# Moving value differences and attention steps within a polysketch-attention and SwiGLU kernel

## The chip, the cores and the metric

The kernel runs on one core of a Trainium2 chip. A core has five engines with instruction queues of their own: TensorE (PE in the profile; its weight loads are listed as PEld), VectorE (DVE), ScalarE (ACT), GpSimd (POOL) and SyncE (SP, which here starts DMA transfers). Each works through its queue in order and waits on semaphores for the others. The metric is the device time of one execution in microseconds (us); lower is better.

## The reference

Two blocks follow each other. The first is attention with a polynomial sketch, over 4 batches, 4 heads, 1088 positions and a head dimension of 32; the second is a SwiGLU feed-forward block over the 4352 resulting tokens of 128 values, with 1536 hidden values.

```python
def phi(x):                                   # 32 values -> 64 features
    a = np.einsum('rd,bhsd->bhsr', S1, x)
    b = np.einsum('rd,bhsd->bhsr', S2, x)
    return np.einsum('bhsi,bhsj->bhsij', a, b).reshape(*x.shape[:-1], r * r)
q_p, k_p = (phi(q), phi(k))
kv = np.einsum('bhsf,bhsd->bhfd', k_p, v)     # per batch and head: 64 x 32
z = np.sum(k_p, axis=2)                       # per batch and head: 64
num = np.einsum('bhsf,bhfd->bhsd', q_p, kv)
den = np.einsum('bhsf,bhf->bhs', q_p, z)[..., None] + 1e-06
x = (num / den)                               # then (B,H,S,D) -> (B*S, H*D)
g = x @ w_gate
out = (g * (1 / (1 + np.exp(-g))) * (x @ w_val)) @ w_out
```

The sums over positions, kv and z, must be complete before any token of a batch is known, so the feed-forward block of a batch can only start when its attention is done.

## The kernel before, in words

**Tiling.** The tokens lie transposed in SBUF (xT, 128 values by 4352 tokens). Each batch is cut into three blocks of 384, 384 and 320 tokens, twelve blocks in all. The hidden dimension is cut into 12 chunks of 128. A *unit* is one block with one chunk: gate and value products, silu, and the multiplication of the two, which leaves one tile in the buffer hbuf. A *down* step (L943) multiplies one such tile by the output weights and adds it to the block's result in PSUM; after 12 of them the result is transposed and stored (L972).

**Stages.** Batch 0 comes first. Its 36 units are plain float32 products (function unit: products L912, silu L918, multiplication L929 on VectorE). Six early ones are *late* units: their value product is copied into hbuf by ScalarE, and the multiplication by the silu follows later on GpSimd (catch_up, L935). The loop over z runs the other thirty units; from z = 17 on, each is followed by a down step and by one part of attention. A closing loop then runs the remaining down steps of batch 0, three to a round, with parts of attention between them (its variable begun becomes true when batch 1's numerators are computed). From there on the *line* loop runs over y, 108 units of batches 1 to 3, with up to two down steps and a part of attention behind each.

**Split products in the line.** In the line the products are split into terms of a faster number format (function cut_unit). The weights are cut in advance by cut_weights, in four pieces of three chunks each, in four rows of steps: *first*, w1 = scaled copy on ScalarE; *low*, low = w - w1 (the value differences, on GpSimd for the value weights); *second*, wb = scaled low on ScalarE; *third*, wd = w1 - wb on GpSimd. All four are recorded at L849. Tokens are cut alike (L859, L860, L864 give x1, x0, xd). A line unit of the first kind then has the products xd by wd (L878), the plain gate product (L880), x1 by w1 (L884) and x0 by wb (L885); ScalarE copies the first scaled (L890), VectorE adds it to the sum of the last two (L893), ScalarE takes the silu (L897) and GpSimd multiplies (L902). From y = 22 (GATES) on the gate is split too; its weights are cut by VectorE in the line's first units.

**Attention of batches 1 to 3.** The generator attentions() yields after each small part, and parts_of(n) runs n parts. In order: transposes of keys (turn_keys, L309) and queries (L560), key sketches (L336), key features (L359), sums of features over the nine position groups (feature_sums, five GpSimd additions at L529, the last of which values() needs), key-value products (values(), L370 and L698 on TensorE), the fold and the spread of the result on VectorE (L583 to L708), query sketches (L324), query features and their transposes (L359, L742), and the numerators (L760), whose result goes to xT (L777). Parts that give TensorE a group of products in the line stand behind a mark "pe"; they run only where GROUPS names the unit y, and group() first runs any part still left before the mark.

**Order and buffers.** The order of instructions on each engine is written out by hand: it is the order of the calls. PSUM has eight banks. In the line one is held for the down steps, and the others go to whichever product comes next, oldest first, so a unit's first product waits for the reader of a bank filled three units before.

**The weights** arrive as 64-bit floats and are converted in 14 pieces; the last step of a piece is a multiplication at L270, on GpSimd for nearly all.

Of the kernel before, what the change touches and what calls it, by code (L numbers as in the profile page):

```python
# [19 lines left out]
def kernel(  # L20
# [126 lines left out]
    def load_k(b):  # L147
        nc.sync.dma_start(
            out=kld[:, 0:NX, :], in_=k[b].rearrange("h (pp x) d -> (h pp) x d", pp=32)
        )  # L150

    def load_q(b, x0=0, x1=NX):
        src = q[b].rearrange("h (pp x) d -> (h pp) x d", pp=32)
        nc.sync.dma_start(out=qld[:, x0:x1, :], in_=src[:, x0:x1, :])

    def load_v(b, queues):
        src = v[b].rearrange("h (pp x) d -> pp h x d", pp=32)
        for a, queue in enumerate(queues):
            n = min(NC, NX - NC * a)
            queue.dma_start(  # L160
                out=vld[32 * a : 32 * a + 32, :, 0:n, :],
                in_=src[:, :, NC * a : NC * a + n, :],
            )
# [620 lines left out]
    todo = []  # L784
# [33 lines left out]
    def cut_weights(w, lows, engine):  # L818

        rows = [], [], [], []  # L820
        sub = dict(op=ALU.subtract)
        for c, (w1, wb, wd) in enumerate(homes(w)):
            src = w[:, 3 * c : 3 * c + 3, :]
            low = lows[c]
            w_parts[id(w), c] = (w1, wb, wd)
            fine = dict(out=wd, in0=whole(w1), in1=whole(wb), **sub), engine.tensor_tensor
            if engine is nc.vector:
                fine = dict(
                    out=wd, in0=low, scalar=-BETA, in1=whole(w1), op0=ALU.mult, op1=ALU.add
                ), engine.scalar_tensor_tensor  # L830
            for row, f, args in zip(
                rows,
                (nc.scalar.activation, engine.tensor_tensor, nc.scalar.activation, fine[1]),
                (
                    dict(out=w1, in_=src, func=AF.Copy, scale=CUT),
                    dict(out=low, in0=src, in1=whole(w1), **sub),
                    dict(out=wb, in_=low, func=AF.Copy, scale=BETA),
                    fine[0],
                ),
            ):  # L840
                row.append((f, args))
        return rows

    def take(steps, n):

        for _ in range(n):
            if steps:
                f, args = steps.pop(0)
                f(**args)  # L849

    def cut_tokens(i, engine=nc.gpsimd):

        t0, n = blocks[i]
        x = xT[:, t0 : t0 + n]
        x1, x0, xd = x_parts[i] = [
            apool.tile([P, BW], F32R, tag=tag, name=name, bufs=2)
            for tag, name in (("qb", "x1"), ("dT", "x0"), ("rd", "xd"))
        ]
        nc.scalar.activation(x1[:, 0:n], x, AF.Copy, scale=CUT)  # L859
        engine.tensor_tensor(  # L860
            out=x0[:, 0:n], in0=x, in1=whole(x1[:, 0:n]), op=ALU.subtract
        )
        yield
        nc.vector.scalar_tensor_tensor(  # L864
            out=xd[:, 0:n], in0=whole(x0[:, 0:n]), scalar=-BETA, in1=whole(x1[:, 0:n]),
            op0=ALU.mult, op1=ALU.add,
        )
# [36 lines left out]
    def unit(i, j, late=False, between=(None, None)):  # L904


        t0, n = blocks[i]
        g, u = bank(), bank()
        for o, w in ((g, wg), (u, wv)):
            if between[0] and w is wv:  # L910
                between[0]()
            nc.tensor.matmul(  # L912
                o[:, 0:n], w[:, j, :], xT[:, t0 : t0 + n], start=True, stop=True
            )
        sg = fpool.tile(
            [P, BW], FP32, tag="sgl" if late else "sg", name="sg", bufs=6 if late else 5
        )
        nc.scalar.activation(sg[:, 0:n], g[:, 0:n], AF.Silu)  # L918
        slot_of[i, j] = slots.pop(0)
        hj = hbuf[:, slot_of[i, j], :]  # L920
        hidden[i, j] = hj
        todo.append((i, j))
        if late:
            if between[1]:
                between[1]()
            nc.scalar.copy(hj[:, 0:n], u[:, 0:n])
            lates.append((hj[:, 0:n], sg[:, 0:n]))
        else:
            nc.vector.tensor_tensor(  # L929
                out=hj[:, 0:n], in0=sg[:, 0:n], in1=u[:, 0:n], op=ALU.mult  # L930
            )

    def catch_up():
        o, sg = lates.pop(0)
        nc.gpsimd.tensor_tensor(out=o, in0=o, in1=sg, op=ALU.mult)  # L935

    def down():

        i, j = todo.pop(0)
        n = SPLIT if i == LAST else blocks[i][1]  # L940
        if j == 0:
            acc[i] = bank("g1" if i == 1 else "acc")
        nc.tensor.matmul(  # L943
            acc[i][:, 0:n],
            wo[:, j, :],
            hidden[i, j][:, 0:n],
            start=(j == 0),
            stop=(j == NCH - 1),
        )
        if i != LAST:  # L950
            hidden.pop((i, j))
            slots.append(slot_of[i, j])
        if j == NCH - 1:
            store(i, n)
# [34 lines left out]
    def part(name, i):  # L989

        next(fills[name, i], None)
# [97 lines left out]
    begun = [False]  # L1089

    def parts_of(n):

        for _ in range(n):
            if ahead[0] not in ("pe", "end"):
                ahead[0] = next(att, "end")
                begun[0] |= ahead[0] == "first"
# [48 lines left out]
    for z, (i, j) in enumerate(seq):  # L1145
        if z == 17:
            free_banks.pop()
            turn[0] %= 4
        unit(i, j)
        for p in parts.get(z, ()):  # L1150
            part(*p)
        if z in (24, 25, 26):
            catch_up()
        if z == 6:
            load_k(1)
            load_v(1, [nc.sync] * 4)
            load_q(1)
        if z >= 17:
            todo.remove(order[0])
            todo.insert(0, order.pop(0))  # L1160
            down()
        if z == 20:
            lows = [
                pool.tile([P, 3, P], FP32, tag=tag, name="low", bufs=bufs)[:]
                for pool, tag, bufs in ((apool, "qb", 2), (apool, "dT", 2), (apool, "rd", 2), (fpool, "sgl", 6))
            ]
            first, low, second, third = cut_weights(wv, lows, nc.gpsimd)
        if 20 <= z < 24:
            take(first, (2, 1, 1, 0)[z - 20])
            take(low, (0, 1, 2, 1)[z - 20])  # L1170
        if z in (25, 26):
            take(second, 2)
        if z >= 17:
            parts_of(1)
        if z == 26:
            take(third, 4)
    todo.sort()
    x_steps = None
    while todo:
        for _ in range(min(3, len(todo))):  # L1180
            down()
        if begun[0]:
            x_steps = x_steps or cut_tokens(HEAD, nc.vector)
            next(x_steps, None)
        parts_of(1 + begun[0] * (1 + (len(todo) < 3)))
    while not begun[0]:
        parts_of(1)
    run(x_steps or cut_tokens(HEAD, nc.vector))
# [4 lines left out]

    line = [3 * b + k for b in range(1, B) for k in ((0, 2, 1) if b == B - 1 else range(3))]
    END = len(line) * NCH
    GROUPS, GATES = (5, 7, 22, 24, 40), 22

    token_steps = {}
    for m, i in enumerate(line[1:], 1):
# [70 lines left out]
```

## Time and profile before

The time is the median of three runs: 295.32 us (295.3 to 296.36). The profiled execution spans 293.6 us.

| engine | busy us | share | instructions |
|---|---|---|---|
| TensorE (PE) | 282.3 | 96% | 2307 |
| VectorE (DVE) | 207.8 | 71% | 422 |
| ScalarE (ACT) | 181.9 | 62% | 432 |
| GpSimd (POOL) | 162.7 | 55% | 183 |

Busy times are of the engine as a whole; they say nothing of the stage that a change touches, so the work around it is read from the order in time. A line of that view gives the start, the duration, the engine, the kernel's line, the operation, the tiles (out<-in), the shape and how many instructions are merged; in square brackets, the idle time before it and the instruction that ended it. A float32 product counts as two instructions of TensorE. The chain of work that ended last lies to 83% on TensorE, 6% on VectorE and 5% on GpSimd. The batch-0 stage ends at about 97.5 us, where the line starts. From 95 to 110 us VectorE is busy for 14.50 of 15 us, from 180 us on TensorE for 109.59 of 113.6.

### The profile page before, as it was taken

How to read it: one execution, taken by the hardware profiler on the slowest of the kernel's cores; microseconds unless marked ns; L12 is line 12 of the kernel's file. 1: busy time of each engine (PE TensorE's matmuls, PEld its weight loads, DVE VectorE, ACT ScalarE, POOL GpSimd, SP SyncE). 2: the span in 40 equal slices, each digit the busy share in tenths (PEclk: the TensorE clock that was granted, in tenths of full speed). 3: DMA queues.
4: the chain of work that ended last, by engine and by line, in shares of the span. 5: the costliest groups of instructions: out<-in, count | busy, mean ns of one | idle time of the engine just before them, and what ended most of it. 6: DMA issues, size and time to landing. Idle time of an engine off the chain costs nothing.

```text
span 293.6 us, 6384 instructions
## 1 busy us (share of the span) xinstructions
PE 282.3 (96%) x2307; PEld 213.0 (73%) x2307; DVE 207.8 (71%) x422; ACT 181.9 (62%) x432; POOL 162.7 (55%) x183
## 2 busy tenths in 40 slices
PE   7899999996999799999999999999999999999994
PEld 6545566654656577767787778888888988888984
DVE  3997988873294996999568875656767666676751
ACT  3567565642301576555467777888888888888860
POOL 3315322269500695689836666557676666665650
PEclk9999999999799999999999999999999999999998
DMA  7563192302221033001001001001001010010101
GB/s 193 151 213 109 57 323 64 125 29 78 73 47 27 17 89 88 2 1 27 7 12 27 2 0 23 3 0 31 0 0 27 2 23 1 2 27 0 22 2 28
DMA packets 26144, 14.34 MB, mean 49 GB/s; under 512 B 19841, under 2 KB 24193, under 8 KB 26113
## 3 DMA queue, kind: packets, MB, share of 16 engines
q1 hardware_dynamic: 25456, 13.84, 18.1%
q8 instruction: 18, 0.29, 0.4%
q10 hardware_dynamic: 656, 0.10, 0.2%
q14 instruction: 14, 0.11, 0.1%
HBM read 11.41 MB, written 2.23 MB: 46 GB/s over the span
## 4 chain that ended last, share of the span: by engine, by line
PE 83%; DVE 6%; POOL 5%; ACT 2%; issue 2%; DMA 2%; SPq 0%; DVEq 0%; ACTq 0%
PE PS L943 25%; PE PS L912 14%; PE PS L884 10%; PE PS L878 10%; PE PS L885 10%; PE PS L880 4%; POOL zs L529 3%; PE PS L336 2%; PE PS L324 2%; PE PS L760 2%; DMA kld<-in_k_dram 2%; ACT sum L890 1%; PE PS L370 1%; DVE sum L893 1%; DVE phk L359 1%
## 5 line engine op out<-in xcount | busy, mean ns | idle before, releaser
L902 POOL TENSOR_TENSOR hbuf<-sg,sum 128x384 f32<-128x384 f32 (+1 forms) x107 | 109.8, 1030 | 58.9 <-ACT sg L897 50.6
L893 DVE SCALAR_TENSOR_TENSOR sum<-PS,sum 128x384 f32<-128x384 f32 (+1 forms) x192 | 93.9, 525 | 46.0 <-ACT sum L890 41.9
L943 PE MATMUL PS<-hbuf,wo 128*128 128x384 f32 (+2 forms) x288 | 103.6, 461 | 0.0
L890 ACT ACTIVATE sum<-PS 128x384 f32<-128x384 f32 (+1 forms) x192 | 80.5, 465 | 14.0 <-PE PS L878 13.6
L943 PEld LDWEIGHTS PS<-hbuf,wo 128*128 128x128 f32 x288 | 52.3, 190 | 10.6 <-issue 0.8
L897 ACT ACTIVATE sg<-sum 128x384 f32<-128x384 f32 (+1 forms) x85 | 42.7, 503 | 26.8 <-DVE sum L893 26.8
L878 PE MATMUL PS<-xd,gphq 128*128 128x384 f32 (+1 forms) x85 | 47.9, 564 | 0.0
L884 PE MATMUL PS<-x,w 128*128 128x384 f32 (+1 forms) x107 | 42.2, 395 | 0.1
L878 PE MATMUL PS<-xd,wd 128*128 128x384 f32 (+1 forms) x107 | 39.4, 368 | 1.8 <-POOL zs L529 1.5
L885 PE MATMUL PS<-x,wb 128*128 128x384 f32 (+1 forms) x107 | 35.0, 327 | 0.0
L918 ACT ACTIVATE sg<-PS 128x384 f32<-128x384 f32 (+1 forms) x37 | 17.4, 473 | 24.5 <-PE PS L912 22.9
L912 PE MATMUL PS<-xT,wg 128*128 128x384 f32 (+1 forms) x74 | 30.1, 489 | 0.0
L912 PE MATMUL PS<-xT,wv 128*128 128x384 f32 (+1 forms) x74 | 29.4, 479 | 0.2 <-DVE wv L270 0.2
L878 PEld LDWEIGHTS PS<-xd,wd 128*128 128x128 f32 x107 | 20.3, 189 | 12.6 <-POOL zs L529 1.7
L884 PE MATMUL PS<-x,graw 128*128 128x384 f32 (+1 forms) x85 | 27.8, 328 | 0.0
L885 PE MATMUL PS<-x,graw 128*128 128x384 f32 (+1 forms) x85 | 27.6, 325 | 0.0
L929 DVE TENSOR_TENSOR hbuf<-sg,PS 128x384 f32<-128x384 f32 (+1 forms) x31 | 16.2, 526 | 12.3 <-PE PS L912 12.0
L884 PEld LDWEIGHTS PS<-x,w 128*128 128x128 f32 x107 | 20.1, 188 | 4.2 <-ACT sum L890 0.4
L878 PEld LDWEIGHTS PS<-xd,gphq 128*128 128x128 f32 x85 | 16.1, 189 | 8.6 <-issue 0.4
L885 PEld LDWEIGHTS PS<-x,wb 128*128 128x128 f32 x107 | 20.2, 188 | 2.9
L912 PEld LDWEIGHTS PS<-xT,wv 128*128 128x128 f32 x74 | 14.1, 194 | 9.4 <-DVE hbuf L929 0.9
L912 PEld LDWEIGHTS PS<-xT,wg 128*128 128x128 f32 x74 | 13.5, 193 | 9.3 <-issue 1.2
(130 smaller groups left out, 345.4 us busy)
## 6 DMA issues: line engine op xcount, KB each, us to landing
kld<-in_k_dram SPq DMA_DIRECT2D x4, 544.0 KB, 4.4
vld<-in_v_dram SPq DMA_DIRECT2D x12, 144.0 KB, 4.8
qld<-in_q_dram SPq DMA_DIRECT2D x3, 544.0 KB, 3.8
raw<-in_moe_w_out_dram SPq DMA_DIRECT2D x4, 384.0 KB, 4.0
out_dram<-o SPq DMA_DIRECT2D x28, 48.0 KB, 1.8
raw<-in_moe_w_gate_dram SPq DMA_DIRECT2D x3, 384.0 KB, 3.2
raw<-in_moe_w_val_dram SPq DMA_DIRECT2D x3, 384.0 KB, 3.4
out_dram<-o SPq DMA_DIRECT2D x16, 40.0 KB, 1.7
```

Of the source, the lines that this page charges most:

```text
L878: nc.tensor.matmul(d, wd, xd, start=True, stop=True)
L880: nc.tensor.matmul(g, wg[:, j, :], xT[:, t0 : t0 + n], start=True, stop=True)
L884: nc.tensor.matmul(p, w1, x1, start=True, stop=False)
L885: nc.tensor.matmul(p, wb, x0, start=False, stop=True)
L890: nc.scalar.activation(s, d, AF.Copy, scale=-1.0 / BETA)
L893: nc.vector.scalar_tensor_tensor(out=s, in0=p, scalar=1.0 + 1.0 / BETA, in1=s, op0=ALU.mult, op1=ALU.add)
L897: nc.scalar.activation(sg, sums[0] if both else g, AF.Silu)
L902: nc.gpsimd.tensor_tensor(out=hj[:, 0:n], in0=sg, in1=sums[-1], op=ALU.mult)
L912: nc.tensor.matmul(o[:, 0:n], w[:, j, :], xT[:, t0 : t0 + n], start=True, stop=True)
L918: nc.scalar.activation(sg[:, 0:n], g[:, 0:n], AF.Silu)
L929: nc.vector.tensor_tensor(out=hj[:, 0:n], in0=sg[:, 0:n], in1=u[:, 0:n], op=ALU.mult)
L943: nc.tensor.matmul(acc[i][:, 0:n], wo[:, j, :], hidden[i, j][:, 0:n], start=(j == 0), stop=(j == NCH - 1),)
```

## The change

Four edits, all of order. No tile, shape or operation changes.

The value differences are rearranged in the last units of the z loop. Before: the first scaled copies at z = 20 to 22, the differences (low) one at z = 21, two at 22, one at 23, the second copies two at z = 25 and two at 26, and all second differences (third) at z = 26. After: the first copies two at z = 20 and two at 21, three differences at z = 21; three second copies at z = 25; the fourth difference at z = 26, behind the last late multiplication; three second differences there; and the fourth second copy and second difference at z = 29. The aim is that the sums of batch 1's features, which stand behind these differences on GpSimd, start sooner.

In the closing loop the last two rounds of down steps each ran three parts of attention; they now run one each. What this leaves over (transposes of keys and queries of later batches, and the sums of batch 2's features) runs in the line's first units, one part behind each, and the first two groups of the line's attention move from units 5 and 7 to 6 and 8. The aim is that the first units' own work on VectorE comes earlier.

```diff
             first, low, second, third = cut_weights(wv, lows, nc.gpsimd)
-        if 20 <= z < 24:
-            take(first, (2, 1, 1, 0)[z - 20])
-            take(low, (0, 1, 2, 1)[z - 20])
-        if z in (25, 26):
-            take(second, 2)
+        if z in (20, 21):
+            take(first, 2)
+        if z == 21:
+            take(low, 3)
+        if z == 25:
+            take(second, 3)
         if z >= 17:
             parts_of(1)
         if z == 26:
-            take(third, 4)
+            take(low, 1)
+            take(third, 3)
+        if z == 29:
+            take(second, 1)
+            take(third, 1)
...
-        parts_of(1 + begun[0] * (1 + (len(todo) < 3)))
+        parts_of(1 + (begun[0] and len(todo) > 2))
...
-    GROUPS, GATES = (5, 7, 22, 24, 40), 22
+    GROUPS, GATES = (6, 8, 22, 24, 40), 22
```

## The prediction

> **What bounds the kernel now.** I read the page first, then the list of waits, then the order in time of each engine round the two waits of TensorE on GpSimd. Times are us from the start of the profile before (the "old clock").
>
> ```profile
> PE 282.3 (96%) x2307; PEld 213.0 (73%) x2307; DVE 207.8 (71%) x422; ACT 181.9 (62%) x432; POOL 162.7 (55%) x183
> PEclk9999999999799999999999999999999999999998
> ```
>
> TensorE is the bound: 282.3 of 293.6. What a change of order can win is its 11.3 us of idle time, and time in which its clock is low: one slice in forty shows a 7.
>
> ```profile
> PE PS L698 <- POOL zs L529: 2.5, 1, 2.5
> PE PS L878 <- POOL zs L529: 1.5, 1, 1.5
> ```
>
> The largest waits of TensorE are the two that the change aims at. The first, in order of time:
>
> ```profile
> 68.00 1.21 PE L370 MATMUL PS<-phk,vld 128*32 128x64 f32 x72
> 71.66 0.32 PE L698 MATMUL PS<-zs,ones 128*32 128x64 f32 x8 [2.45 <-POOL zs L529]
> 71.91 1.27 PE L336 MATMUL PS<-s,kT 128*64 128x64 f32 x36
> 73.11 1.44 PE L912 MATMUL PS<-xT,wg 128*128 128x320 f32 x2
> 74.34 1.27 PE L912 MATMUL PS<-xT,wv 128*128 128x320 f32 x2
> 75.41 1.38 PE L943 MATMUL PS<-hbuf,wo 128*128 128x384 f32 x2
> 76.72 1.69 PE L324 MATMUL PS<-s,qT 128*32 128x96 f32 x72
> ```
>
> TensorE ends the key-value products of batch 1 at 69.2 and stands still for 2.45. The three pairs from 73.11 then take 3.61; the same pairs take 0.64 + 0.54 + 0.64 = 1.82 five us later (78.34 to 80.16). The stretches say why (third column from the end: clock):
>
> ```profile
> 73.00:74.00 1.00, 1.00 (x9) 0.73 (x5) 0.77 (x2) 0.00 (x0) 1.00 (x2) 0.57 0.00 0
> 75.00:76.00 1.00, 1.00 (x3) 0.55 (x2) 0.28 (x1) 0.02 (x1) 1.00 (x2) 0.50 0.16 33
> 77.00:78.00 1.00, 1.00 (x61) 1.00 (x56) 0.00 (x0) 0.18 (x1) 0.35 (x1) 1.00 0.11 22
> ```
>
> Half clock from about 73.1 to 76.5, right behind the standstill. What GpSimd did ahead of it:
>
> ```profile
> 57.00 1.01 POOL L849 TENSOR_TENSOR low<-wv,w 128x384 f32<-128x384 f32 x1
> 61.37 1.00 POOL L270 TENSOR_TENSOR wo<-man,exp 128x384 f32<-128x384 f32 x1 [3.36 <-DVE man L261]
> 62.33 2.92 POOL L849 TENSOR_TENSOR low<-wv,w 128x384 f32<-128x384 f32 x3
> 65.20 1.01 POOL L935 TENSOR_TENSOR hbuf<-hbuf,sg 128x384 f32<-128x384 f32 x1
> 66.16 2.51 POOL L529 TENSOR_TENSOR zs<-phk 128x512 f32<-128x512 f32 x2
> ```
>
> It idles 3.36 before the conversion of the last output weights, then does three value differences ahead of the feature sums. The second wait:
>
> ```profile
> 97.25 1.76 DVE L359 TENSOR_TENSOR phk<-kab 128x512 f32<-128x512 f32 x1
> 98.94 1.42 DVE L309 STREAM_TRANSPOSE kT<-kld 128x640 f32<-128x640 f32 x2
> 100.69 1.39 DVE L560 STREAM_TRANSPOSE qT<-qld 128x640 f32<-128x640 f32 x2
> 102.01 0.98 DVE L893 SCALAR_TENSOR_TENSOR sum<-PS,sum 128x384 f32<-128x384 f32 x2
> ```
>
> The view names GpSimd here, but L878 at 102.67 (fourth unit of the line, U3) writes a bank that the first unit's sum (L893) must have read; that sum was ready at 98.9 and ran at 102.01, behind five instructions of attention. So this wait is VectorE's order, 1.46 us.
>
> **What the Trainium skill says.** "TensorE: Matmul & The Clock Gate", Part 1, "What's actually happening": the array falls to half clock after an idle window of about 3.4 us and returns after a busy one; the windows run freely. The trace agrees: 3.4 us at half clock. Same page, "Architectural detail": ACT and DVE are strict FIFO; the late sum shows it. "GPSIMD Engine Reference", 1 "Specifications": its SBUF interface is shared with VectorE instructions that have two SBUF inputs. The trace agrees: the 128x512 key features took 0.68 with GpSimd still, and 1.76 beside a feature sum.
>
> **Part 1: differences one unit sooner.** No instruction is added or removed; the order on ScalarE and GpSimd changes. Differences 2 and 3 move ahead of the L270 conversion. Their inputs (L849 on ScalarE) are done at 56.0 and 56.95, so they run at 57.97 and 58.95 in the idle 3.36, free. L270 still starts at 61.37 (its input comes at 61.28), and the late multiplication L935 follows at 62.33, not 65.20. Features for the sums are ready at 62.47 and 63.54, in time. From L935's start to the last sum's end the old order took 71.61 - 65.20 = 6.41; so 62.33 + 6.41 = 68.74, and TensorE asks at 69.2: the 2.45 goes whole, with 0.46 to spare. Behind it TensorE sets the pace to 97.5: the fold on VectorE, the query sketches and the numerators (16 down products of 10 us hide the feature chain; it ended 1.9 before TensorE asked) all move with it. With the standstill gone, the small products last 68.0 to 70.65; the like stretch at 105.2 to 107.6 ran at full clock. So the half clock goes too: 3.61 - 1.82 = 1.79. **Sum 4.24.** Bounds: 2.45 if the clock dips anyway, 4.24 if not; I take 4.24.
>
> The fourth difference, its ScalarE scaling and its second difference move behind the late multiplications: about 70.6, 76.6 and 77.1. Their reader is the tenth unit of the line, past 110, and GpSimd idled 19.68 there: nothing. The fourth scaling on ScalarE sits in its 11.43 of idle before the numerators: nothing.
>
> **Part 2: fewer parts in the last rounds, groups one unit later.** The last two rounds ran 3 + 3 parts and now run 1 + 1; key and query transposes and feature sums spread over the line's units 0 to 2. On the old clock (all of it now 4.24 earlier): the first feature sum on GpSimd now waits for the last key features. These end at 97.95 (0.68 instead of 1.76, GpSimd being still). VectorE goes on: output transpose 0.47 to 98.4, keys 0.80 to 99.15, sum U0 0.55 to 99.7, keys 0.7, sum U1 to 100.85, queries 0.8, gate difference 0.85 (L849), sum U2 to 102.85. U3 finds its bank at 101.06, so the 1.46 goes. U3, U4, U5 at 1.17 each (98.72 to 99.89 is one) end at 104.57; the key-value products (1.03) end at 105.6.
>
> There a **new wait** begins. Sums of features and multiplications (L902) alternate on GpSimd: sum 98.05 to 99.4; multiplication to 100.8; sum 1.3 to 102.1; multiplication 1.0; sum 1.3 to 104.4; multiplication 1.0 to 1.3; sums 0.72 + 0.72: ends at 106.9 to 107.3. And L336 of the group now waits for the sum of U5: from 102.85, queries 0.62, gate 0.85, then three times sum and gate (0.47 + 0.85, pipelined) less the last gate, about 107.3. So TensorE idles 1.3 to 1.7 at L698, L336 starts at about 107.45 and unit U6 at 107.45 + 1.2 = 108.65. The old U6 started at 108.89. **Gain 0.24**, not 1.46: VectorE was busy 14.50 of 15 from 95 to 110, so it, not the one wait, sets this stage. Bounds: if gate differences run as L860 does beside a still GpSimd (0.56), 4 x 0.3 less, U6 at 107.5, gain 1.3; if multiplications take 1.34 as at 103.3, loss 0.3. From U8 on (114.7) both orders have done the same products.
>
> Batch 2's feature and query parts then come one unit (1.82) later against the line, and the third group stays at unit 22. Feature sums end about 139.5, asked for at 143.0; the last query transpose ends about 139.5, asked for at 140.48: hidden. The sum of unit 21, whose bank L760 takes, ended at 140.56 and now follows that transpose, a sum and an xd (0.55 to 1.05): 140.2 to 141.5. Loss 0 to 0.9; I take 0.3.
>
> **Sum:** 4.24 + 0.24 - 0.3 = 4.2; 295.3 - 4.2 = **291.1**.
>
> **Rivals.** *The clock follows the new wait* (16%): 1.3 to 1.7 idle among 2.4 us of small products is near what came before the dip at 73 (2.45 idle); a further 1.8 is lost: 292.9. For it: nearness. Against: 1.46 idle at 101.2 left the clock at 1.00. *VectorE gains more* (8%): 291.1 less 1.1, 290.0. For it: the key features save 1.08 by a still GpSimd. Against: GpSimd is busy beside the gate differences. *No change* (7%): the clock dips at 73 all the same and both losses reach their ends, 295.3 - 2.45 + 0.3 + 0.9 = 294.1. *Slower* (5%): multiplications between the sums take 1.72 each (the slowest L902), U6 comes 2.1 later, half clock there and at 73 too, 0.9 at unit 22: 295.3 - 2.45 + 2.1 + 1.8 + 0.9 = 297.7. For it: the sums now really stand behind multiplications that wait for VectorE. Against: everything must go wrong at once. My forecast: 64%.
>
> **How the numbers follow.** The time is the forecast's. The range takes in its bounds (4.24 + 1.3 gives 289.8; 0.3 and 0.9 lost gives 292.3) and the clock rival at 292.9: 289.9 to 293.1. Faster by over 0.5% means below 293.8: 64 + 16 + 8 = 88%; same 7%; slower 5%.
>
> **What would show it.** No wait of L698 near 67 to 69 and no 7 in the clock's row; L912 pairs behind it at 0.54 to 0.64; key features at 0.68 each near 93; no wait of L878 near 97; instead about 1.5 of L698 on GpSimd near 101, and under 1 at L760 near 136. Wrong if the clock still halves for 3.4 us in either place, or if the new wait at L698 is over 2.5.

## The result, and the profile after

The changed kernel takes **291.88 us** (median of four runs: 291.78, 291.84, 291.92 and 293.83), the kernel before 295.31 (four runs beside them, 294.97 to 296.36). The ratio is 0.9894, 95% interval 0.9846 to 0.9941. The profiled execution spans 289.9, before 293.6. "Old clock", U0, U1 and so on, "first group" (L370, L698, L336) and "second group" (L324) are used as in the prediction; "third group" is the L370 at unit 22.

The page of the kernel after, its busy times and clock row:

```profile
PE 280.7 (97%) x2307; PEld 212.4 (73%) x2307; DVE 207.1 (71%) x422; ACT 181.5 (63%) x432; POOL 162.7 (56%) x183
PEclk9999999999999999999999999999999999999999
```

The 7 has gone from the clock row. TensorE's busy time fell by 1.6 for the same 2307 instructions, about what the half clock had cost. The list of waits of the kernel after still has one of 2.3 at L698:

```profile
PE PS L698 <- POOL zs L529: 2.3, 1, 2.3
```

But it is not the one of before. TensorE in order of time, where the old wait stood:

```profile
67.65 1.21 PE L370 MATMUL PS<-phk,vld 128*32 128x64 f32 x72
68.68 0.29 PE L698 MATMUL PS<-zs,ones 128*32 128x64 f32 x8
68.91 1.27 PE L336 MATMUL PS<-s,kT 128*64 128x64 f32 x36
70.10 0.81 PE L912 MATMUL PS<-xT,wg 128*128 128x320 f32 x2
70.75 0.70 PE L912 MATMUL PS<-xT,wv 128*128 128x320 f32 x2
71.28 0.81 PE L943 MATMUL PS<-hbuf,wo 128*128 128x384 f32 x2
```

No bracket stands at L698: the list shows no wait of it. The three pairs start 0.65 and 0.53 apart, and the next product starts at 72.02: 1.92 in all, where they took 3.61. GpSimd ahead of it, kernel after:

```profile
56.64 2.91 POOL L849 TENSOR_TENSOR low<-wv,w 128x384 f32<-128x384 f32 x3
61.01 1.00 POOL L270 TENSOR_TENSOR wo<-man,exp 128x384 f32<-128x384 f32 x1 [1.46 <-DVE man L261]
61.98 1.00 POOL L935 TENSOR_TENSOR hbuf<-hbuf,sg 128x384 f32<-128x384 f32 x1
...
67.67 0.73 POOL L529 TENSOR_TENSOR zs<-zs,phk 128x256 f32<-128x256 f32 x1
```

Three differences in one row fill part of the idle time, which was 3.36 and is now 1.46; the last sum ends at 68.40, 0.28 before L698 starts.

The new wait is in the line. TensorE, kernel after:

```profile
100.62 1.21 PE L370 MATMUL PS<-phk,vld 128*32 128x64 f32 x72
104.16 0.32 PE L698 MATMUL PS<-zs,ones 128*32 128x64 f32 x8 [2.33 <-POOL zs L529]
104.41 1.27 PE L336 MATMUL PS<-s,kT 128*64 128x64 f32 x36
```

Points on the way split the span:

| from the profiles, us | before | after |
|---|---|---|
| U0 starts (L878) | 97.48 | 92.78 |
| U0 to U8 | 17.22 | 18.92 |
| of it U0 to U6 | 11.41 | 12.83 |
| U8 to the third group | 27.28 | 27.18 |
| third group to the last row of products (L958) | 144.34 | 144.33 |

So 4.70 is gained before the line (0.36 of it by loads that came sooner in this execution, ahead of everything that was changed), 1.70 is given back in the line's first eight units, and behind them nothing moves. The last products come 3.1 sooner; the other 0.6 of the span lies behind the last copy (o_last, at 289.63 and at 286.52), in the last transfers: 4.0 before, 3.4 after. What follows asks why the line gave back 1.7.

### The profile page after: what moved, and what is told of

Its sections match the earlier page's. It is cut to its first block, busy times and chain, and to the rows that moved or that the text cites. A ratio compares the mean times of both kernels' runs of the same rounds, so it can differ in the third digit from the quotient of the medians.

```text
span 289.9 us, 6382 instructions
## 1 busy us (share of the span) xinstructions
PE 280.7 (97%) x2307; PEld 212.4 (73%) x2307; DVE 207.1 (71%) x422; ACT 181.5 (63%) x432; POOL 162.7 (56%) x183
## 3 DMA queue, kind: packets, MB, share of 16 engines
HBM read 11.41 MB, written 2.23 MB: 47 GB/s over the span
## 4 chain that ended last, share of the span: by engine, by line
PE 84%; DVE 6%; POOL 3%; ACT 2%; issue 2%; DMA 1%; SPq 0%; DVEq 0%; POOLq 0%; ACTq 0%
PE PS L943 26%; PE PS L912 16%; PE PS L884 10%; PE PS L878 10%; PE PS L885 10%; PE PS L880 4%; PE PS L336 2%; PE PS L324 2%; PE PS L760 2%; POOL zs L529 2%; DVE sum L893 1%; DMA kld<-in_k_dram 1%; ACT sum L890 1%; PE PS L370 1%; POOL hbuf L902 1%
## 5 line engine op out<-in xcount | busy, mean ns | idle before, releaser
L902 POOL TENSOR_TENSOR hbuf<-sg,sum 128x384 f32<-128x384 f32 (+1 forms) x107 | 109.4, 1025 | 61.4 <-ACT sg L897 51.2
L893 DVE SCALAR_TENSOR_TENSOR sum<-PS,sum 128x384 f32<-128x384 f32 (+1 forms) x192 | 93.9, 526 | 48.3 <-ACT sum L890 42.1
L878 PE MATMUL PS<-xd,gphq 128*128 128x384 f32 (+1 forms) x85 | 47.9, 564 | 0.0
L878 PE MATMUL PS<-xd,wd 128*128 128x384 f32 (+1 forms) x107 | 39.4, 369 | 0.7 <-DVE sum L893 0.4
L912 PE MATMUL PS<-xT,wg 128*128 128x384 f32 (+1 forms) x74 | 29.5, 480 | 0.0
L912 PE MATMUL PS<-xT,wv 128*128 128x384 f32 (+1 forms) x74 | 28.8, 471 | 0.2 <-DVE wv L270 0.2
L878 PEld LDWEIGHTS PS<-xd,wd 128*128 128x128 f32 x107 | 20.3, 189 | 11.5 <-DVE sum L893 1.2
L878 PEld LDWEIGHTS PS<-xd,gphq 128*128 128x128 f32 x85 | 16.1, 189 | 8.6 <-issue 0.4
```

The costliest lines, as they stand in the source:

```text
L878: nc.tensor.matmul(d, wd, xd, start=True, stop=True)
L893: nc.vector.scalar_tensor_tensor(out=s, in0=p, scalar=1.0 + 1.0 / BETA, in1=s, op0=ALU.mult, op1=ALU.add)
L902: nc.gpsimd.tensor_tensor(out=hj[:, 0:n], in0=sg, in1=sums[-1], op=ALU.mult)
L912: nc.tensor.matmul(o[:, 0:n], w[:, j, :], xT[:, t0 : t0 + n], start=True, stop=True)
```

## The experiments

Each kernel was timed beside the kernel before, and its ratio is to that.

### The two parts by themselves

Part 1 alone is the kernel after with two lines as before:

```diff
-        parts_of(1 + (begun[0] and len(todo) > 2))
+        parts_of(1 + begun[0] * (1 + (len(todo) < 3)))
-    GROUPS, GATES = (6, 8, 22, 24, 40), 22
+    GROUPS, GATES = (5, 7, 22, 24, 40), 22
```

> Part 1 alone: the value differences moved, the closing loop and the groups as before. Theory A (part 1 is the whole gain, and part 2 costs about 1.6 us at the first group of the line): no wait of L698 and no half clock near 70, U0 of the line about 4.3 sooner, the old 1.46 us wait of L878 back, no wait of L698 in the line; 290.3 to 291.0 us. Theory B (part 2 brings what it was meant to, and part 1 less than it seems): 293.0 us or more.

Measured: **290.52** (290.22 to 291.66), ratio 0.9851 (0.9812 to 0.9891). U0 starts at 93.33, and U0 to U8 takes 17.23 as before. In its first units GpSimd does all five sums in a row. The wait at L878 stays; its line names GpSimd, but as in the kernel before, the product follows VectorE's sum of U0 (L893, from 97.86). TensorE, then GpSimd, of part 1 alone:

```profile
98.52 0.42 PE L878 MATMUL PS<-xd,wd 128*128 128x384 f32 x1 [1.45 <-POOL zs L529]
```

```profile
96.30 2.09 POOL L529 TENSOR_TENSOR zs<-zs 128x512 f32<-128x512 f32 x2
98.47 0.73 POOL L529 TENSOR_TENSOR zs<-zs,phk 128x256 f32<-128x256 f32 x1
99.16 5.18 POOL L902 TENSOR_TENSOR hbuf<-sg,sum 128x384 f32<-128x384 f32 x4
```

The sums are done at 99.20, then come the multiplications (L902). Part 1 is the whole gain: without part 2 the kernel is no slower.

Part 2 alone is the kernel before with those two lines as after.

> Part 2 alone: the value differences as before, fewer parts in the last rounds and groups at units 6 and 8. Theory A: the 2.45 us wait and the half clock at 68 to 77 are there, and the first group of the line waits over 2 us for the feature sums; 296.5 to 297.2 us, slower than before. Theory B: 293.8 us, faster than before by the 1.46 us of the wait of L878.

Measured: **297.13** (296.11 to 298.0), ratio 1.0052 (1.0023 to 1.0082): part 2 makes the kernel slower. Its fourteen runs fall into two heaps, seven at 296.1 to 296.6 with a mean clock of 0.994 and seven at 297.7 to 298.0 with 0.988. The profile is of the second kind; the first group's wait of 2.33 is followed by half clock. TensorE, and the stretches round it (third column from the end: clock):

```profile
108.61 0.32 PE L698 MATMUL PS<-zs,ones 128*32 128x64 f32 x8 [2.33 <-POOL zs L529]
```

```profile
105.00:110.00 5.00, 2.67 (x117) 2.34 (x116) 4.91 (x11) 1.08 (x3) 4.92 (x6) 1.00 0.35 111
110.00:115.00 5.00, 5.00 (x19) 3.39 (x13) 1.11 (x3) 2.25 (x6) 3.89 (x4) 0.66 0.11 24
```

The first of the two rows also shows VectorE (4.91 of 5) and GpSimd (4.92) full round L698.

### The two edits of part 2 apart

Part 1 with the closing loop of after alone:

> Part 1 and, of part 2, the fewer parts in the last rounds alone; the groups stay at units 5 and 7. If the groups' later place is what makes the alternating sums bearable: L698 waits 3 to 4 us for the feature sums, which end near 104 whatever TensorE does; 293.0 us, or near 295 where the clock halves behind it. If the place does not matter: 291.9 us as the changed kernel.

Measured: **295.03** (294.35 to 296.09), ratio 0.9982 (0.9963 to 1.0002). The sums lie between multiplications as in the kernel after, and the group asks a unit sooner. On TensorE:

```profile
99.67 1.21 PE L370 MATMUL PS<-phk,vld 128*32 128x64 f32 x72 [0.39 <-DVE sum L893]
104.56 0.44 PE L698 MATMUL PS<-zs,ones 128*32 128x64 f32 x8 [3.69 <-POOL zs L529]
104.93 2.19 PE L336 MATMUL PS<-s,kT 128*64 128x64 f32 x36
```

A wait of 3.69, then half clock at once (2.19 for products that take 1.27), in every one of its fourteen runs, to judge by their mean clock (0.994 or less).

Part 1 with the groups of after alone:

> Part 1 with the first two groups of the line's attention one unit later (6 and 8), and the closing loop as before. Theory A (what part 2 loses comes from the closing loop, which puts the feature sums behind the line's multiplications; the place of the group alone costs nothing when the sums are early): no wait of L698 in the line, the wait of 1.45 at L878 stays, U0 to U8 about 17.2, and 290.3 to 290.8, as for part 1 alone (290.52). Rival B (the later groups are what costs, since batch 2's features and queries then stand later against the line): a wait of 0.5 or more ahead of the third group at unit 22 or within the groups, and 291.3 to 292.

Measured: **291.2** (291.01 to 291.46), ratio 0.985 (0.9811 to 0.9889). In its profile the group's place does cost something: U0 to U8 takes 17.95, 0.72 more than with part 1 alone, of which 0.47 shows as a wait of L336 for VectorE's sum of the unit before it:

```profile
103.76 1.27 PE L336 MATMUL PS<-s,kT 128*64 128x64 f32 x36 [0.47 <-DVE sum L893]
```

The kernels with the old line (before, part 1 alone, and the filled one below) agree to 0.01 in this distance, so 0.72 is clear of noise there. The medians differ by 0.7 as well, but the ratios (0.985 and 0.9851) do not. So the two edits belong together: the later group costs up to 0.7, and keeps the loop's edit from costing 4.5; with both, 1.4 is lost.

### Are the multiplications between the sums the cause?

The kernel after with all five sums of batch 2 issued to GpSimd ahead of the line:

```diff
-        yield from beside(turn_keys(3), sums)
-        yield from beside(turn_queries(2), sums)
+        while sums:
+            sums.pop(0)()
+        yield from turn_keys(3)
+        yield from turn_queries(2)
```

> The changed kernel, with batch 2's five feature sums all issued ahead of the line, right behind the features, and only the transposes left in the units 0 to 2. Theory A1 (the group waits because the sums alternate with the multiplications on GpSimd, and nothing else): the sums end near 99, L698 does not wait, U6 starts about 2 us sooner; 289.8 us. Theory A2 (VectorE's queue sets it as well): L698 does not wait, but L336 of the group then waits for the sum of U5, which ran at 103.45 in the changed kernel; U6 starts at most 0.5 us sooner; 291.4 to 291.9 us.

Measured: **291.08** (290.83 to 292.54), ratio 0.9863 (0.9822 to 0.9904). The wait of L698 is gone, but the next product of the group has one of its own (TensorE; this kernel's lines stand 2 further down):

```profile
103.48 1.27 PE L336 MATMUL PS<-s,kT 128*64 128x64 f32 x36 [1.86 <-DVE sum L895]
```

VectorE's sum of U5 ends at 103.43. In the kernel after it ends at 103.99 and GpSimd's last sum at 104.11: two queues end the stage at nearly the same time, and taking one away shows the other. In this execution the clock halved behind the wait of 1.86; it is the 292.54, the only one of seven.

The same with the gate differences (VectorE, L849) moved behind the group, and the two later rows of gate steps with them:

```diff
-            if y >= (0, 1, 5, 5)[n]:
+            if y >= (0, 5, 6, 7)[n]:
```

> The changed kernel with the feature sums issued ahead of the line, and the gate differences on VectorE moved from units 1 to 4 to units 5 to 8 (and the steps behind them to 6 to 10). If VectorE's queue is what the first group waits for: no wait of L336 over 0.3 us, U6 1.6 us sooner. Whether that stays a gain is what the run decides: the moved 3.5 us meet the features of batch 3 at units 9 to 13, where the sum of unit 14 came only 0.6 us ahead of need. Gain kept: 289.5 us; moved into waits of L878 at units 14 to 18: 290.5 to 291.5 us.

Measured: **290.69** (290.45 to 292.08), ratio 0.9837 (0.9809 to 0.9865). The first group has no wait left and U0 to U8 takes 15.71, 1.5 less than before. But U8 to the third group takes 29.08 instead of 27.2. The stretch from 105 to 135 (behind its length: busy PE, PEld, DVE, ACT, POOL) has VectorE busy for 27.29 of 30 us, against 24.30 in the kernel after, and TensorE waits twice for it (0.35 and 0.46):

```profile
105.00:135.00 30.00, 29.18 (x177) 20.11 (x176) 27.29 (x41) 16.91 (x36) 21.23 (x18) 1.00 0.13 29
```

So VectorE's queue did bound the first group; but the work put off fills it up to unit 22 and is waited for there.

### GpSimd and VectorE beside each other

The prediction let the last key features run alone on VectorE (0.68). In the kernel after they took, on VectorE and GpSimd:

```profile
92.55 1.77 DVE L359 TENSOR_TENSOR phk<-kab 128x512 f32<-128x512 f32 x1
97.65 1.08 DVE L849 TENSOR_TENSOR hbuf<-wg,graw 128x384 f32<-128x384 f32 x1
99.75 1.50 DVE L849 TENSOR_TENSOR hbuf<-wg,graw 128x384 f32<-128x384 f32 x1
```

```profile
92.34 1.43 POOL L529 TENSOR_TENSOR zs<-phk 128x512 f32<-128x512 f32 x1 [14.15 <-DVE phk L359]
96.06 1.01 POOL L902 TENSOR_TENSOR hbuf<-sg,sum 128x384 f32<-128x384 f32 x1 [2.29 <-ACT graw L849]
97.03 1.28 POOL L529 TENSOR_TENSOR zs<-phk 128x512 f32<-128x512 f32 x1
98.28 1.32 POOL L902 TENSOR_TENSOR hbuf<-sg,sum 128x384 f32<-128x384 f32 x1
99.56 1.27 POOL L529 TENSOR_TENSOR zs<-zs 128x512 f32<-128x512 f32 x1
103.19 0.92 POOL L529 TENSOR_TENSOR zs<-zs,phk 128x256 f32<-128x256 f32 x1
```

The ends of these rows show how the two engines meet. The gate difference of 1.08 ends at 98.73, 0.42 after the sum that was running when it started (98.31); the one of 1.50 ends at 101.25, 0.42 after its sum (100.83); the two that follow, of 0.89 and 0.61, end 0.41 and 0.42 after theirs, and the key features 0.55 after the first sum (93.77). In the kernel before, the four gate differences also end 0.41 or 0.42 after a GpSimd instruction. So such a VectorE instruction is not slowed in proportion: to judge by these rows it waits for the rest of the GpSimd instruction, however long that is, and then needs 0.42, or 0.55 for 128x512. That is some 0.13 less than the whole operation takes while GpSimd is still (0.55 at 128x384, the L864 at 92.08; 0.69 at 128x512, below).

The first sum starts at 92.34, when only the third of the four pieces of key features is there, and runs beside the fourth. It may: it adds position groups 0 and 1 to 4 and 5. To keep it off, the first two sums change places, so that the first needs the last piece:

```diff
-            lambda: add(s[:, 0:2, :], rows[:, 0:2, :], rows[:, 4:6, :]),
             lambda: add(s[:, 2:4, :], rows[:, 2:4, :], rows[:, 6:8, :]),
+            lambda: add(s[:, 0:2, :], rows[:, 0:2, :], rows[:, 4:6, :]),
```

On the kernel after with its sums first:

> The changed kernel with the feature sums issued ahead of the line and in the other order. Theory E: the last key features 0.68 us, the wait of L336 for the sum of U5 0.8 instead of 1.86 us, clock at 1.00; 290.0 us against 291.1 with the sums issued first in the old order. Theory F: 291.1 us.

Measured: **290.31** (290.21 to 290.87), ratio 0.9821 (0.9793 to 0.9848). VectorE, then TensorE, of this kernel:

```profile
93.30 0.69 DVE L359 TENSOR_TENSOR phk<-kab 128x512 f32<-128x512 f32 x1
```

```profile
103.39 1.27 PE L336 MATMUL PS<-s,kT 128*64 128x64 f32 x36 [1.36 <-DVE sum L895]
```

The features fall from 1.76 to 0.69, the wait from 1.86 to 1.36, the time by 0.8. The intervals of the two ratios overlap, but the rows of the profiles leave no doubt that the sum held up the features, and that this lies on the path.

On part 1 alone:

> Part 1 alone, with the first two feature sums in the other order, so that the first one issued needs the last key features and GpSimd starts its sums only when VectorE has done with them. Theory E (the last key features take 1.76 instead of 0.68 us because a feature sum on GpSimd runs beside them, and VectorE's queue sets this stage): 0.68 us for them, the sums of units 1.08 us sooner, the wait of L878 0.3 to 0.5 instead of 1.45 us, the feature sums end no later; 289.4 us against 290.5 of part 1 alone. Theory F (the order of the queue alone sets it, and the contention costs nothing on the path): 290.5 us or more.

Measured: **290.59** (289.19 to 291.84), ratio 0.9824 (0.9791 to 0.9857). L878's wait falls from 1.45 to 0.38 and the features take 0.69, but the time stays at that of part 1 alone. TensorE shows where the gain went:

```profile
100.95 1.09 PE L336 MATMUL PS<-s,kT 128*64 128x64 f32 x29
103.01 0.45 PE L336 MATMUL PS<-s,kT 128*64 128x64 f32 x7 [0.97 <-issue]
```

It stands for 0.97 in the middle of one group of products and waits for nothing that the profile shows. One execution more of the same kernel:

> The same kernel as part 1 with the two feature sums swapped, once more, for a second profile. If the 0.97 in which TensorE stood inside L336 without a wait that the profile shows was chance, this profile lacks it: U0 to U6 10.6 (11.58 less 0.97) and about 289.6. If the order causes it, it stands at the same place again, and the time is 290.5.

Measured: 290.13, and TensorE stands for 0.68 at the same product. So it wasn't chance; but it need not be in every run, since the fastest of the six above (289.19) is as fast as the kernel without it further down.

### The stand inside L336

The queue list of the transfers gave a lead. In the kernel with the swapped sums, between 100.5 and 101.0, just behind the load of batch 3's queries (544 KB, the transfer engines full from 99.5 to 100), goes a packet of the instruction queue (packets, MB, share of the engines' time):

```profile
q8 instruction: 1, 0.02, 12.0%
q1 hardware_dynamic: 6, 0.01, 4.7%
```

With part 1 alone, which doesn't stand there, the packet goes between 99.0 and 99.5, ahead of that load. Two kernels move the load, which follows batch 2's query transposes. In the first it stands behind all transfers of the spread:

```diff
-            if x1 == 4 * NC and b + 1 < B:
+            if x1 == 4 * NC and b + 1 < B and b != 2:
                 load_q(b + 1)
...
             spread = spread_out(b, kv)
+            if b == 2:
+                load_q(3)
```

> Part 1 with the two feature sums swapped, and the load of batch 3's queries (544 KB) issued behind the first group's spread instead of behind batch 2's query transposes. Theory F (the 0.7 to 1.0 in which TensorE stands inside L336 is a late block of its instructions, which comes over the same DMA engines behind that load): the instruction queue's packet goes before 100 us, the stand is gone, U0 to U6 about 10.6 to 10.8, and 289.6 to 290.0. Rival G (the load has nothing to do with it): it stands 0.7 to 1.0 at the same place, and 290.3 to 290.7. Should the load come too late for batch 3's query transposes, VectorE waits for it after the second group, and TensorE at the third.

Measured: 292.78 (292.02 to 294.29), ratio 0.9898 (0.9861 to 0.9936). The packet goes between 98 and 99, the stand is gone, and U0 to U8 takes 16.14, the 1.1 less that the swap should bring. But the load was issued at 109.04, and VectorE waits for it ahead of the transposes:

```profile
113.89 0.85 DVE L560 STREAM_TRANSPOSE qT<-qld 128x640 f32<-128x640 f32 x1 [3.90 <-DMA qld<-in_q_dram]
```

U8 to the third group takes 30.80. In the second, with the same line at L560, the load goes between the first and the second pair of the spread's transfers:

```diff
             nc.sync.dma_start(out=spread[m:P, s, :], in_=spread[0 : P - m, 0, :])
+            if b == 2 and s == 1:
+                load_q(3)
```

> As the run before, but the load of batch 3's queries is issued between the first and the second pair of the spread's transfers (about 103.7 instead of 109.0), so that it lands about 108, ahead of batch 3's query transposes at about 110. Theory F (TensorE's stand in L336 is an instruction block behind that load): no stand, U0 to U6 10.3 to 10.8, U0 to U8 about 16.1 as with the late load, no wait of VectorE for the load, and from U8 to the third group 27.2 as in the other kernels; so 1.0 to 1.1 below part 1 alone: 289.2 to 289.8. Rival H (the part of the batch behind the first group is bounded by VectorE whatever comes before): U8 to the third group takes 28 or more and 290.2 to 290.7.

Measured: **289.43** (289.2 to 289.63), ratio 0.979 (0.9758 to 0.9822), the fastest kernel of the study and the one with the least scatter. TensorE of it:

```profile
100.90 0.29 PE L698 MATMUL PS<-zs,ones 128*32 128x64 f32 x8
101.12 1.27 PE L336 MATMUL PS<-s,kT 128*64 128x64 f32 x36
102.32 0.44 PE L880 MATMUL PS<-xd,wd 128*128 128x384 f32 x1
```

No wait, no stand; U0 to U8 16.14 (17.37 and 17.08 in the two profiles with the stand), U8 to the third group 27.29. That the place of the query load decides whether TensorE stands is shown by the profiles (the intervals of the ratios overlap); that it does so by way of the late instruction packet is the reading that fits them all, but no run moved the packet by itself.

### What the half clock is worth, and what brings it

The kernel before, with eleven small products of constants (L225) between the key-value products and L698, so that TensorE works while it waits for GpSimd:

```diff
         key_values(kv[:, 0:F], phk, 0, NC)
+        if fill is not None:
+            keep_warm(11, ps=fill)
...
```

> The kernel before, with 11 products of constants (bf16, 512 columns, some 0.2 us each, result unused) put between the key-value products and the products with the feature sums of batch 1, where TensorE stands still for 2.45 us. The wait for GpSimd stays. Theory C (the half clock from 73 to 76.5 follows from the standstill): the clock stays at 1.00, the three pairs behind it take 1.8 instead of 3.6; 293.5 us. Theory D (the dip has another cause, such as the small products themselves): the dip stays, 295.3 us or more.

Measured: **293.8** (293.44 to 295.41, 22 runs), ratio 0.9954 (0.9936 to 0.9972). TensorE:

```profile
68.87 2.56 PE L225 MATMUL PS<-const-bfloat16-1.0 128*32 128x512 bf16 x11
71.50 0.32 PE L700 MATMUL PS<-zs,ones 128*32 128x64 f32 x8
...
72.95 0.81 PE L914 MATMUL PS<-xT,wg 128*128 128x320 f32 x2
73.59 0.70 PE L914 MATMUL PS<-xT,wv 128*128 128x320 f32 x2
74.13 0.81 PE L945 MATMUL PS<-hbuf,wo 128*128 128x384 f32 x2
```

L698 (here L700) still comes at 71.50, with GpSimd's last sum, but the pairs behind it run at full clock. Between the medians lie 1.5. In the profiles U0 comes at 95.63 instead of 97.48; 0.16 of these 1.85 was there ahead of the filler (L370 at 67.84 instead of 68.00), so the half clock alone is worth 1.7.

## Why the prediction came out, and where it was wrong

The forecast was 291.1, the measurement 291.88. Step by step:

**Part 1, the wait of 2.45 and the half clock behind it: right in mechanism and size.** Predicted 4.24; U0 came 4.70 sooner, 4.34 less the 0.36 of earlier loads. (The kernels with part 1 start U0 between 92.78 and 93.54, so a single profile gives it to about 0.4.) From L935's start to the last sum's end the prediction had 6.41; it was 6.42 (61.98 to 68.40). The choice of 4.24 over 2.45 was right as well: with full clock behind it, all of it came, and the filled kernel confirms the 1.7 (predicted 1.79) that belong to the clock alone. The Trainium skill, "TensorE: Matmul & The Clock Gate", Part 1, "What's actually happening", puts the drop behind an idle window of about 3.4 us. The prediction took its trace to agree; the length of the drop (3.4) does, the idle time ahead of it does not: here standstills of 2.33 and 2.45 were enough, though not in each execution. Small products stood round them; whether these count as idle no run shows.

**The fourth difference: right.** TensorE never waits for these pieces: none of its waits in the list of the kernel after names L849.

**Part 2, the first group: wrong in sign.** Predicted a gain of 0.24 (U6 at 108.65 instead of 108.89), measured a loss of 1.42 to U6 and 1.70 to U8; 290.52 with part 1 alone against 291.88 says the same in time, though the intervals of the two ratios overlap. The form was foreseen: a new wait of L698 on sums that alternate with multiplications, VectorE as what bounds the stage. The term that failed is the length. The prediction put the wait at 1.3 to 1.7; it was 2.33, though TensorE asked 0.75 later than walked (L370 at 105.32 on the old clock, not 104.57). L698 then started at 108.86 on the old clock, not at 106.9 to 107.3. Three terms of the walk were too short:

- "The first feature sum on GpSimd now waits for the last key features", which would end after 0.68. It didn't wait: it needs other position groups, and started ahead of them at 92.34. They took 1.77. That is 1.1 on VectorE, ahead of all its work of the line; the swap of two sums gave it back (0.69), and 0.8 of time. The profile before shows the same: this sum started at 97.03, the last features at 97.25, so nothing made it wait there either.

```profile
97.03 1.43 POOL L529 TENSOR_TENSOR zs<-phk 128x512 f32<-128x512 f32 x1 [19.68 <-DVE phk L359]
```

- Gate differences at 0.85: the first three took 1.08, 1.50 and 0.89, beside sums and multiplications of GpSimd.
- The first multiplication was walked to end at 100.8; on the old clock it only started then (96.06 + 4.70), after 2.29 of idle time. Its line names ScalarE, but the silu was done at 94.37; the multiplication also reads VectorE's sum of U0, which ended at 95.91, on the old clock 0.9 later than walked (100.61 for 99.7) because of the features ahead of it. So this follows from the first point. From the end of this multiplication to the end of the last sum the walk had 6.1 to 6.5; it took 7.0, with multiplications of 1.32 for 1.0 and last sums of 1.04 and 0.92 for 0.72.

The Trainium skill, "GPSIMD Engine Reference", 1 "Specifications", which the prediction cited, was right that the two engines share an interface for such operands; the prediction applied it to the key features the wrong way round, because it didn't see which position groups the first sum reads.

**The wait of 1.46 at L878: right.** It fell to 0.40 (U5's), and this alone gained nothing; the prediction had said that VectorE, not the one wait, sets the stage. From 100 to 105 VectorE is busy for 4.94 and GpSimd for 4.92 of 5.

**The third group: the 0.3 didn't come.** U8 to the third group takes 27.18 instead of 27.28.

**The sum.** Without the 0.36 at the start and the 0.6 behind the last product, the profiles give 4.34 - 1.70 + 0.10 = 2.7 instead of 4.2: the forecast's 0.8 of error would have been 1.5, if the two executions had begun and ended alike. The medians (3.43) lie between. So a part of the closeness is luck.

**The rivals.** "The clock follows the new wait" came true in part: the run of 293.83, one in four, at a clock of 0.994, and at least seven of fourteen with part 2 alone. That "1.46 idle left the clock at 1.00" held in every profile; 2.33 was on the edge. (The 1.46 stood between large products, the 2.33 among small ones, so the comparison that the prediction drew on was not a close one.) "VectorE gains more" and "No change" did not come. "Slower" needed everything at once, and indeed a group one unit sooner (3.69 of wait, half clock) nearly brought it: 295.03.

What stays open is the scatter of one kernel. Of 87 runs of the kernel before that stood beside the experiments, 49 have a mean clock of 0.994 or less (median 296.40). The twelve at 1.000 have a median of 293.8, like the filled kernel, but the 26 between lie at 294.5 to 296.5, so a part of the scatter is not in the mean clock. Part 1 alone also has runs at 290.3 and at 291.4 with full clock. The end of the program is one place for it: behind the last copy the filled kernel also took 4.0, part 1 and part 2 alone 3.2 and 3.3, with the same transfers. A stand like that in L336 is another. No run tested either. And the 4.34 is what is gained over an execution with half clock, which the profile of before was (mean clock 0.991): the median of part 1 alone lies 5.9 below the 49 runs and 3.3 below the twelve.

## What to carry to other kernels

When a step is moved so that two engines work at the same time, read from the code which rows each instruction takes and thus what really holds it back, and cost a VectorE operation with two SBUF inputs by what is left of the GpSimd instruction that runs when it starts. When a change has two parts, cost each by the distance between fixed points of the timeline (here U0, U8, the third group): the gain of one hid the loss of the other, and part 1 alone came out faster (290.52 against 291.88). Where a removed wait gains nothing, look for the next thing that holds the same stretch; here it was another queue, and then a large load whose issue could move.

## What was not expected of the hardware

- **TensorE can stand without a wait that the profile shows.** 0.97 and 0.68 inside a row of like products, in the kernel whose instruction packet came behind a load of 544 KB; moving the load took it away and gave 1.2 (290.59 to 289.43).
- **Half clock came after less idle time than the 3.4 us of the page cited above, and not always.** 1.45 between large products: in no profile. Among small ones, 1.36: in none of five runs (sums swapped). 1.86: one run of seven. 2.33: one of four (after) and at least seven of fourteen (part 2 alone, the seven at 0.988; of the other seven one can't say which of the two waits it was). 2.45: 49 of the 87 runs of before. 3.69: all fourteen. (These counts are by the mean clock of a run, which doesn't say where it fell: one run each of the swapped sums on part 1 alone and of the filled kernel also has 0.994.) A longer standstill was followed by half clock more often; why the same one sometimes is and sometimes isn't, no run shows.
- **VectorE waits out GpSimd, it isn't just slowed.** Operations of VectorE with two SBUF inputs ended 0.41 to 0.42 (128x384) or 0.55 (128x512) after the GpSimd instruction that ran when they started. Key features on 128x512 so took 0.69 alone and 1.77 beside a sum; gate differences on 128x384 0.55 to 1.50. GpSimd pays less: its multiplications in the line's first units took 1.01, and 1.32 where such an operation of VectorE ended in them.
